# Windowed attention with global tokens and a gated MLP on one core: 512-token chunks, one chunk of all global tokens, clipped band matmuls, denominators from ones columns and exp(-ln), loads in the order of first use

## The chip, the cores and the metric

The kernel runs on one core of one Trainium2 chip. The metric is device time in microseconds (us) of one execution. Each execution has a state (fast or slow); only fast runs are compared. The engines are PE (TensorE: matmuls), PEld (PE's weight loads), DVE (VectorE), ACT (ScalarE), POOL (GpSimd, which also issues the casting loads) and SP (SyncE, which issues plain DMAs).

## The reference, cut to what matters

Eight batches of eight heads. 512 local tokens attend within 32 positions and to 32 global tokens; the global tokens attend to everything. An MLP with the gate h * clip(h + 3, 0, 6) / 6 follows on all 8 x 544 = 4352 tokens.

```python
batch, n_heads, seq_l, seq_g, head_dim = (8, 8, 512, 32, 64)
n_tokens, d_model, d_ff = (4608, 512, 2048)       # w_in 512x2048, w_out 2048x512
k_all = np.concatenate([k_g, k_l], axis=2); v_all = np.concatenate([v_g, v_l], axis=2)
out_g = np.matmul(sm(scale * np.matmul(q_g, k_all.transpose(0, 1, 3, 2))), v_all)
mask = np.abs(pos[:, None] - pos[None, :]) <= 32
s_ll = np.where(mask, scale * np.matmul(q_l, k_l.transpose(0, 1, 3, 2)), -1e9)
s_lg = scale * np.matmul(q_l, k_g.transpose(0, 1, 3, 2))
out_l = np.matmul(sm(np.concatenate([s_lg, s_ll], -1)), np.concatenate([v_g, v_l], axis=2))
x = concat([out_g, out_l], axis=2), tokens in rows # 4352 x 512
h = x @ w_in;  y = (h * np.clip(h + 3.0, 0.0, 6.0) / 6.0) @ w_out
```

## The kernel before

A pair of heads goes through transposes of q and k, QK by key block of 128, exp on ACT, masks on DVE, and the value matmuls ("AV"). The MLP of the batch before is cut into pieces (`fill()`) and put between. Cuts are marked `# ...`.

The value matmuls take all 512 columns of a zero-padded band tile, and two of the seven per head have only 32 rows (the global keys). The kernel splits 544 tokens into a 512-column matmul and a second, 32-column one (`pavB`, here and `psB` below):

```python
def emit_head_av(b, h8, gkE, par):
    # ...
    for kb in range(NKB):
        nc.tensor.matmul(out=pavA[0:MW, 0:SB], lhsT=vn[kb][:, vcol:vcol + MW],
                         rhs=etile[par][kb][:, e * S:e * S + SB], start=(kb == 0), stop=False)
    nc.tensor.matmul(out=pavA[0:MW, 0:SB], lhsT=vg[0:Sg, vcol:vcol + MW],
                     rhs=gkE[0:Sg, 0:SB], start=False, stop=True)
    nc.tensor.matmul(out=pavB[0:MW, 0:SR], lhsT=vn[NKB - 1][:, vcol:vcol + MW],
                     rhs=etile[par][NKB - 1][:, e * S + SB:e * S + S], start=True, stop=False)
    nc.tensor.matmul(out=pavB[0:MW, 0:SR], lhsT=vg[0:Sg, vcol:vcol + MW],
                     rhs=gkE[0:Sg, SB:S], start=False, stop=True)
```

One ones column of `vn` gives the softmax denominator as one row. It is transposed, inverted, transposed back, written to DRAM and read back broadcast over 64 partitions; every second head's result then takes one more DMA to its place:

```python
    nc.vector.transpose(out=dt[D:D + 32, :], in_=xtu[D:D + 32, :])
    nc.vector.reciprocal(out=dt16[...][:, :, 0:1], in_=dt[...][:, :, 0:1])
    nc.vector.transpose(out=rec[D:D + 32, :], in_=dt16[D:D + 32, :])
    nc.sync.dma_start(out=rscr[gi:gi + 1, :], in_=rec[D:D + 1, 0:S])
    # ... later:
    nc.sync.dma_start(out=rbc, in_=rscr[gi:gi + 1, :].to_broadcast([D, S]))
    nc.vector.tensor_tensor(out=xth[:, 0:S], in0=rbc, in1=xtu[0:D, 0:S], op=mult)
    nc.sync.dma_start(out=st["xt"][hp][D:2 * D, 0:S], in_=xth[:, 0:S])
```

The MLP runs per batch over 544 tokens. The second layer has five token tiles, the last of 32 tokens:

```python
for m_ in range(NP):                                    # first layer, 16 column blocks c
    nc.tensor.matmul(out=psA[:, 0:SB], lhsT=lhs, rhs=st["xt"][m_][:, 0:SB], ...)
    nc.tensor.matmul(out=psB[:, 0:SR], lhsT=lhs, rhs=st["xt"][m_][:, SB:S], ...)
# ... relu and gate, once for psA and once for psB
for c in range(NDFF):                                   # second layer, NTS = 5 token tiles
    nc.tensor.matmul(out=po[0:ntok, 0:dm], lhsT=gts[c][:, t0:t0 + ntok], rhs=w_out_t[c], ...)
```

All weights are loaded ahead of batch 0's q, k and v, on one queue (POOL's).

The softmax here doesn't subtract the row's maximum and nothing guards it: scores larger than these inputs give would overflow.

## Time and profile before

| | before |
|---|---|
| median of 4 executions | 566.08 us (564.65 to 577.32; the highest counts as slow, 2.2% above the fastest; the mean of the other three is 565.6) |
| profiled execution: span, mean granted PE clock | 567.9 us, 0.930 |
| first PE matmul | 38.5 us |
| PE idle after that | 57.5 us |

The page gives each engine's busy time and share; its clock row is PE's granted clock in tenths of full speed, in 40 slices.

```profile
span 567.9 us, 9070 instructions
...
PE 471.9 (83%) x3072; PEld 222.2 (39%) x3072; DVE 345.3 (61%) x913; ACT 274.8 (48%) x705; POOL 168.8 (30%) x408
...
PEclk9999969999797997989699997979979998999799
```

PE is the busiest engine by far. The waits view (engine, waiting instruction, what it waited for: us in total, times, longest) says where PE stood still, with the long first wait on top:

```profile
PE psq L173 <- DMA qgb<-in_q_g_dram: 38.5, 1, 38.5
PE psA L304 <- DMA xt_5522<-xth: 5.8, 1, 5.8
PE psA L304 <- DMA xt_2954<-xth: 2.6, 1, 2.6
```

The `xt` waits come at the end of the reciprocal's trip through DRAM: the first MLP matmuls of a batch need the last pair's result. There is one such wait in nearly every batch.

PE's timeline (start us, duration us, engine, line, output<-inputs, weight rows*columns, moving shape) during one head's value matmuls. Going from a matmul with 128 weight rows to one with 32, or back, is called a tiling change below. Durations overlap, so read the distance from one start to the next:

```profile
248.52 0.38 PE L249 MATMUL pavA<-E_0_107,vn_2059 128*96 128x512 f16 x1
...
249.16 0.38 PE L249 MATMUL pavA<-E_3_113,vn_2083 128*96 128x512 f16 x1
249.47 0.41 PE L252 MATMUL pavA<-gkE,vg 32*96 32x512 f16 x1
249.82 0.22 PE L254 MATMUL pavB<-E_3_113,vn_2083 128*96 128x32 f16 x1
249.96 0.21 PE L257 MATMUL pavB<-gkE,vg 32*96 32x32 f16 x1
250.11 0.39 PE L326 MATMUL po<-wout_153,gt_2634 128*128 128x512 f16 x1
250.33 0.38 PE L326 MATMUL po<-wout_155,gt_2650 128*128 128x512 f16 x1
```

512-wide matmuls follow each other at 0.215 us. Around the 32-row ones it is different: 249.16 to 249.47 is 0.31, 249.47 to 249.82 is 0.35, and the two 32-wide ones take 0.14 and 0.15 us.

Last, the windows view (stretch, length, busy us and count of PE, PEld, DVE, ACT, POOL, then PE's clock, DMA share, GB/s). PE falls to half clock after a thin stretch (attention with no MLP work between; even so, no gap between PE's matmuls from 60 us to there is longer than 0.8 us) and stays there for some 9 us although it is 100% busy:

```profile
76.00:78.00 2.00, 2.00 (x6) 0.69 (x5) 1.17 (x3) 1.97 (x7) 1.32 (x9) 0.50 1.90 136
...
80.00:82.00 2.00, 2.00 (x9) 0.94 (x9) 1.97 (x7) 0.67 (x2) 0.00 (x0) 0.50 0.23 60
```

I summed this over the whole trace in windows of 2 us. "Clock loss" is PE's busy time times (1 - clock), and "full-clock busy" is what is left. PE's idle time is the span less the time to the first PE work and less PE's busy time.

| kernel | span | first PE work | PE idle after it | clock loss | full-clock busy |
|---|---|---|---|---|---|
| before | 567.9 | 38.5 | 57.5 | 34.7 | 437.2 |

### The profile page before, as it was taken

The page shows a single profiled execution, that of the slowest core. Times are in us where ns is not written, and L with a number is a line of the kernel's source. Part 1 is how long each engine was busy: PE and PEld are TensorE (multiplying, and loading weights), DVE is VectorE, ACT ScalarE, POOL GpSimd, SP SyncE. Part 2 cuts the span into 40 slices and gives each one's busy share as a digit, 9 for nine tenths or more (in the row PEclk, how much of TensorE's full clock was granted, in tenths as well). Part 3 has the DMA queues.
Part 4 walks back from the last instruction along what each step waited for, and adds up shares of the span by engine and source line. Part 5 has one row for each costly group of instructions (what it writes and reads, how often), then busy time and mean ns, then how long its engine had stood idle before and what let it go on. Part 6 is the DMA issues. An engine that isn't in the chain of part 4 may idle for free.

```text
span 567.9 us, 9070 instructions
## 1 busy us (share of the span) xinstructions
PE 471.9 (83%) x3072; PEld 222.2 (39%) x3072; DVE 345.3 (61%) x913; ACT 274.8 (48%) x705; POOL 168.8 (30%) x408
## 2 busy tenths in 40 slices
PE   0028898998798987999988987989979988999597
PEld 0013444444343443444444443434434443444243
DVE  9004787846684476853778466843868546873551
ACT  0016857706583076813577075830758156840350
POOL 8796741605133051511316051330511011010000
PEclk9999969999797997989699997979979998999799
DMA  6999990926139260861609260391600110002001
GB/s 108 198 152 75 89 85 21 95 71 64 25 30 85 76 55 16 62 68 64 51 21 96 70 64 25 37 89 65 56 20 17 57 38 25 16 30 70 17 20 61
DMA packets 122095, 33.83 MB, mean 60 GB/s; under 512 B 108928, under 2 KB 117184, under 8 KB 122048
## 3 DMA queue, kind: packets, MB, share of 16 engines
q0 software_dynamic: 109248, 17.57, 41.3%
q1 hardware_dynamic: 12800, 15.68, 9.1%
q8 instruction: 24, 0.39, 0.3%
q14 instruction: 23, 0.19, 0.1%
HBM read 39.58 MB, written 8.98 MB: 86 GB/s over the span
## 4 chain that ended last, share of the span: by engine, by line
PE 55%; DVE 19%; DMA 12%; ACT 7%; POOL 4%; issue 2%; SPq 0%; POOLq 0%; ACTq 0%; DVEq 0%
PE po L326 25%; PE pavA L249 10%; PE psA L304 10%; DMA rbc<-rscr 7%; DVE rec L273 4%; PE pavA L252 3%; DVE dTh_140 L267 2%; DMA rscr<-rec 2%; DVE xth L289 2%; DMA win_151<-in_moe_w_in_dram 2%; ACT etmp L212 1%; ACT kT L189 1%; ACT qT L180 1%; PE psGA L226 1%; PE pavB L254 1%
## 5 line engine op out<-in xcount | busy, mean ns | idle before, releaser
L180 ACT COPY qT<-psq 128x544 f16<-128x544 f16 x32 | 19.6, 612 | 136.5 <-PE psq L176 136.5
L219 POOL COPY E_0_107<-etmp 128x32 f16<-128x32 f16 x32 | 9.1, 283 | 234.3 <-ACT etmp L212 234.0
L329 DVE COPY ot<-po 128x512 f32<-128x512 f32 (+1 forms) x40 | 27.6, 689 | 83.6 <-PE po L326 83.6
L173 PE MATMUL psq<-ident,qgb 32*128 32x32 f16 x32 | 5.9, 183 | 38.5 <-DMA qgb<-in_q_g_dram 38.5
L233 ACT ACTIVATE gkE<-psGA 32x512 f16<-32x512 f32 x64 | 36.2, 576 | 0.0
L216 DVE TENSOR_TENSOR E_0_107<-etmp,mask_95 128x192 f16<-128x192 f16 x32 | 8.1, 254 | 39.9 <-issue 27.2
L252 PE MATMUL pavA<-gkE,vg 32*96 32x512 f16 x64 | 28.6, 446 | 0.0
L304 PEld LDWEIGHTS <-win_151 128*128 128x128 f16 x128 | 13.2, 103 | 38.0 <-DMA xt_5522<-xth 6.1
L273 DVE STREAM_TRANSPOSE rec<-dTh_1_143 32x544 f16<-32x544 f16 x32 | 23.2, 726 | 0.8
L273 DVE STREAM_TRANSPOSE rec<-dTh_0_141 32x544 f16<-32x544 f16 x32 | 23.1, 723 | 0.6
L204 PEld LDWEIGHTS <-kT 64*128 64x128 f16 x256 | 11.2, 95 | 25.6 <-ACT kT L189 18.1
L173 PEld LDWEIGHTS <-qgb 32*128 32x128 f16 x32 | 3.4, 105 | 45.0 <-DMA qgb<-in_q_g_dram 38.5
L304 PEld LDWEIGHTS <-win_147 128*128 128x128 f16 x128 | 13.4, 105 | 18.1 <-issue 5.2
L304 PEld LDWEIGHTS <-win_149 128*128 128x128 f16 x128 | 13.2, 103 | 18.2 <-issue 5.2
L189 ACT COPY kT<-psk 128x544 f16<-128x544 f16 x32 | 19.9, 620 | 0.2
L263 ACT COPY xtu_133<-pavA 65x512 f32<-65x512 f32 x8 | 4.7, 582 | 31.6 <-PE pavA L252 31.6
L154 POOL DMA_DIRECT2D qgb<-in_q_g_dram x8 | 4.8, 598 | 47.2 <-PE psq L176 47.2
L252 PEld LDWEIGHTS <-vg 32*96 32x96 f16 x64 | 7.6, 119 | 28.2 <-issue 28.2
L208 PEld LDWEIGHTS <-kT 64*128 64x128 f16 x256 | 14.4, 103 | 9.1 <-issue 8.9
L219 POOL COPY E_0_115<-etmp 128x32 f16<-128x32 f16 x32 | 8.7, 273 | 30.8 <-ACT etmp L212 30.7
L304 PEld LDWEIGHTS <-win_145 128*128 128x128 f16 x128 | 12.7, 99 | 11.6 <-issue 2.5
L226 PE MATMUL psGA<-qT,kT 64*32 64x512 f16 x64 | 14.1, 436 | 0.0
(1772 smaller groups left out, 1777.0 us busy)
## 6 DMA issues: line engine op xcount, KB each, us to landing
out_dram<-ot SPq DMA_DIRECT2D x32, 256.0 KB
rbc<-rscr SPq DMA_DIRECT2D x64, 68.0 KB
rscr<-rec SPq DMA_DIRECT2D x64, 1.1 KB
win_145<-in_moe_w_in_dram POOLq DMA_DIRECT2D x1, 512.0 KB, 5.8
win_147<-in_moe_w_in_dram POOLq DMA_DIRECT2D x1, 512.0 KB, 5.3
win_149<-in_moe_w_in_dram POOLq DMA_DIRECT2D x1, 512.0 KB, 6.6
win_151<-in_moe_w_in_dram POOLq DMA_DIRECT2D x1, 512.0 KB, 8.5
out_dram<-ot SPq DMA_DIRECT2D x8, 64.0 KB
```

The source lines that it names most:

```text
L180: nc.scalar.copy(out=qT, in_=psq[:, 0:S])
L189: nc.scalar.copy(out=kT, in_=psk[:, 0:S])
L208: nc.tensor.matmul(out=psS[e][:, c0 + Sg:c0 + BW], lhsT=lhs, rhs=qT[e * D:(e + 1) * D, Sg + F[kb]:Sg + F[kb] + FR])
L219: nc.gpsimd.tensor_copy(out=etile[par][kb][:, e * S:e * S + Sg], in_=etmp[:, c0:c0 + Sg])
L226: nc.tensor.matmul(out=psGA[e][0:Sg, 0:SB], lhsT=kT[e * D:(e + 1) * D, 0:Sg], rhs=qT[e * D:(e + 1) * D, 0:SB])
L233: nc.scalar.activation(out=gkE[0:Sg, 0:SB], in_=psGA[e][0:Sg, 0:SB], func=EXP, scale=qk_scale)
L249: nc.tensor.matmul(out=pavA[0:MW, 0:SB], lhsT=vn[kb][:, vcol:vcol + MW], rhs=etile[par][kb][:, e * S:e * S + SB], start=(kb == 0), stop=False)
L252: nc.tensor.matmul(out=pavA[0:MW, 0:SB], lhsT=vg[0:Sg, vcol:vcol + MW], rhs=gkE[0:Sg, 0:SB], start=False, stop=True)
L273: nc.vector.transpose(out=rec[D:D + 32, :], in_=dt16[D:D + 32, :])
L304: nc.tensor.matmul(out=psA[:, 0:SB], lhsT=lhs, rhs=st["xt"][m_][:, 0:SB], start=(m_ == 0), stop=(m_ == NP - 1))
L326: nc.tensor.matmul(out=po[0:ntok, 0:dm], lhsT=gts[c][:, t0:t0 + ntok], rhs=w_out_t[c], start=(c == 0), stop=(c == NDFF - 1))
L329: nc.vector.tensor_copy(out=ot[0:ntok, :], in_=po[0:ntok, 0:dm])
```

## The change

The intent: take columns and instructions off PE, take the DRAM trip out of the chain, and start earlier. The diff replaces nearly the whole body; this is its core (cuts marked).

```diff
-        for kb in range(NKB):
-            nc.tensor.matmul(out=pavA[0:MW, 0:SB], ..., rhs=etile[par][kb][:, e * S:e * S + SB], ...)
-        nc.tensor.matmul(out=pavA[0:MW, 0:SB], lhsT=vg[0:Sg, ...], rhs=gkE[0:Sg, 0:SB], ...)
+            # vgz: all 128 rows, zero outside the head's 32; columns 64..127 are ones
+            nc.tensor.matmul(out=pav[:, 0:Sl], lhsT=vgz[:, b, h], rhs=EG[:, 0:Sl], start=True, ...)
+            nc.tensor.matmul(out=pg[:, m, e], lhsT=vgz[:, b, h], rhs=EG[:, Sl:S], start=True, ...)
+            for kb in range(NT):
+                lo, w = WIN[kb]                         # w is 160 or 192
+                nc.tensor.matmul(out=pav[:, lo:lo + w], lhsT=vn[b % NV][:, kb, h],
+                                 rhs=E[:, e, half, COL[kb]:COL[kb] + w], ...)
+                nc.tensor.matmul(out=pg[:, m, e], lhsT=vn[b % NV][:, kb, h],
+                                 rhs=E[:, e, half, g0:g0 + Sg], ...)
-        nc.vector.transpose(...); nc.vector.reciprocal(...); nc.vector.transpose(...)
-        nc.sync.dma_start(out=rscr[gi:gi + 1, :], in_=rec[D:D + 1, 0:S])    # and back, broadcast
+            nc.scalar.activation(out=Ln[e * D:(e + 1) * D], in_=pav[D:P, 0:Sl], func=LN)
+        nc.scalar.activation(out=Rc, in_=Ln, func=EXP, scale=-1.0)
+            nc.vector.tensor_tensor(out=xts[b][m][r], in0=Rc[r], in1=pavs[e][0:D, 0:Sl], op=mult)
# ...
+    emit_globals(0)                                   # globals: loaded once, transposed once
+    for p in range(NPAIR):
+        # T(p + 2), QK(p + 1), AV(p), with 8 MLP units between them
+        if m == NM - 1:
+            units += moe_units(lambda mm, b=b: xts[b][mm], Sl, ...)           # 512 tokens
+    units += moe_units(lambda mm: xg[mm].rearrange("p b s -> p (b s)"), B * Sg, ...)  # 256 globals
# ... loads: k, q of heads 0 to 3, globals, v, the other heads, batch 1, w_in, w_out;
# ... DVE fills vn (ones), kgz and vgz (zeros) before it casts the globals
```

64 ones columns in the value weights give each denominator on 64 PSUM partitions, so no broadcast is needed.

## The prediction

> **What bounds it now.** TensorE. The page's busy table gives PE 83%, DVE 61%, ACT 48%. The waits view: PE's first matmul waits 38.5 us for the q_g load, which is issued after all the weights; later PE waits are short (2 to 6 us per batch for xt after the reciprocal's round trip through DRAM; all PE idle after the start is about 57 us). The windows view shows clock 0.50 in stretches (75 to 85, 175 to 180 us) that follow thin attention phases or waits; the mean is 0.93, so about 30 us are lost to it.
>
> Start-to-start distances in PE's timeline at full clock: 512-wide matmuls 0.216 us; the 32-wide psB one only 0.03; 0.14 to 0.34 where the row tiling changes (a 32-row gkE matmul followed by a 128-row one: 0.34 instead of 0.22). The Trainium skill, TensorEngine Tiling, Key Properties, says that changing the mode drains the engine; the trace agrees with about 0.1 us. Sum: po 640 x 0.216 = 138; psA/psB 126; AV 64 x 1.6 = 102; transposes, QK, G 32 x 1.8 = 58. Together 424 us, + 38 start + clock 30 + gaps = 568.
>
> **What changes on PE (estimates from those distances).**
> - MoE: 8 chunks x 27.7 + one 256-token global chunk 14 = 235 us, instead of 264.
> - AV: one 512-wide, four 160/192-wide, five 32-wide matmuls per head, all 128 rows: about 0.7 us, 45 us in all (was 102).
> - Transposes 0.5, QK 0.65 with its mode changes, G 0.28 per pair: 46 us (was 58).
> Sum about 326: 98 us fewer, all on the limiting engine.
>
> **Other engines.** The DRAM round trip, vector transposes, reciprocals and POOL copies go. Added per pair: two Ln and one Exp (about 0.5 us each by the spacing of 512-wide ACT work), masks 352 wide. With 8 first-layer units, a pair costs about 8.6 us on ACT, 7.8 on DVE, 9.8 on PE: still PE-bound, but ACT is near. Stalls: 10 us.
>
> **Start.** DVE zeroes and fills vn, kgz, vgz before the global casts that PE's first instruction needs. The Trainium skill, VectorE: DVE Perf Modes, Zero memsets, says one cycle per element; the trace of before has no large memset to test it. That is about 19 us of memsets and 5 of ones (estimate from that page), after masks at about 10 us: PE starts at about 30 us. The v_g loads wait for the vgz memsets, and batch 1's loads and w_in queue behind them on POOL (0.9 us each 1024-row load). Batch 0 has no MoE to fill with: ACT-bound, 4 x 4.5 us plus prologue. First MoE matmul at about 58 us.
>
> **Sum.** 58 + 7 batches x 39.5 + tail (last batch 27.7, globals 14, ends 4) + stalls 10 = about 390 us, 0.69 of before. Range 368 to 424. Faster by over 2%: 0.98; within 2%: 0.01; slower: 0.01.
>
> **Right or wrong would show as:** PE busy share over 85% from 60 us to the end, clock near 1.0 there; pair period about 9.8 us in the timeline; AV distances 0.03 for the 32-wide matmuls and 0.07 to 0.08 for the band ones (if weight loads limit them, nearer 0.06 and 0.10: +10 us); PE's first wait released by DVE's casts or memsets at about 30 us; no PE waits on xt from DMA.
>
> **What could be wrong:** memsets two or four times faster than one element per cycle (−8 to −12 us); PSUM's seven shared buffers or the in-order Ln/Exp/multiply chain stalling PE in first-layer stretches (+20 to +30 us); the clock falling to 0.5 there; the dependency tracking making the first transposes wait for all heads' loads (+5 us); late weights (+5 to +15 us).

## The result, and the profile after

| | before | after |
|---|---|---|
| median of 4 executions | 566.08 us | 375.88 us (375.38 to 376.71) |
| profiled span, clock | 567.9 us, 0.930 | 375.0 us, 0.986 |

The ratio is 0.6645, 95% interval 0.6628 to 0.6662. A ratio here is the mean time of one kernel's fast runs over that of the other's in the same rounds, so it is not quite the ratio of the medians. The prediction of 390 us, range 368 to 424, holds.

The page after, the same lines:

```profile
span 375.0 us, 6707 instructions
...
PE 332.3 (89%) x2608; PEld 178.9 (48%) x2608; DVE 235.6 (63%) x489; ACT 239.5 (64%) x473; POOL 102.6 (27%) x132
...
PEclk9998969999999999999999999999999999999999
```

PE's clock row now shows dips only in its first six slices. PE's waits after:

```profile
PE psGT L190 <- DVE kgn_192 L183: 20.1, 1, 20.1
PE pg L286 <- DVE xg_199 L314: 4.7, 6, 0.8
PE psH L324 <- DMA win_86<-in_moe_w_in_dram: 2.1, 1, 2.1
```

No wait on `xt` from DMA is left. The first wait is released by DVE, at 20.1 us. One head's value matmuls in PE's timeline after:

```profile
107.82 0.38 PE L284 MATMUL pav<-EG,vgz 128*128 128x512 f16 x1
108.03 0.18 PE L286 MATMUL pg<-EG,vgz 128*128 128x32 f16 x1
108.06 0.23 PE L292 MATMUL pav<-E,vn_83 128*128 128x160 f16 x1
108.13 0.18 PE L295 MATMUL pg<-E,vn_83 128*128 128x32 f16 x1
108.16 0.24 PE L292 MATMUL pav<-E,vn_83 128*128 128x192 f16 x1
...
108.44 0.18 PE L295 MATMUL pg<-E,vn_83 128*128 128x32 f16 x1
108.47 0.38 PE L324 MATMUL psH<-xt_732,win_84 128*128 128x512 f16 x1
```

From 107.82 to 108.47 a head takes 0.65 us, where it took about 1.6 before (248.52 to 250.11 for the head shown). Band matmuls are 0.07 to 0.08 apart, and the 32-wide ones, with a full weight load each, only 0.03. Two windows, batch 0's attention and one steady batch:

```profile
23.00:45.00 22.00, 16.56 (x221) 11.59 (x217) 13.06 (x34) 21.19 (x55) 18.05 (x26) 0.92 1.58 143
...
85.00:125.00 40.00, 38.49 (x312) 20.46 (x311) 25.92 (x57) 28.47 (x55) 10.51 (x12) 1.00 0.69 67
```

Batch 0, with no MLP to fill with, is bound by ACT (21.19 of 22 us). In the steady batch PE is busy for 38.49 of 40 us at full clock. The second layers of successive batches start 40.2 us apart (70.4, 110.6, 150.8 us).

| kernel | span | first PE work | PE idle after it | clock loss | full-clock busy |
|---|---|---|---|---|---|
| before | 567.9 | 38.5 | 57.5 | 34.7 | 437.2 |
| after | 375.0 | 20.1 | 22.6 | 4.7 | 327.6 |
| difference | 192.9 | 18.4 | 34.9 | 30.0 | 109.6 |

The four differences add up to the gain: 57% of it is full-clock busy time of PE, the rest is waiting, half clock and the start. Full-clock busy is not work alone. The experiment a7 below runs the same 2608 matmuls as the kernel after, and its full-clock busy is 11.5 us higher, in batches that have more waits. So up to some 10 us of the 109.6 may be of that kind and not work taken away.

### The profile page after: what moved, and what is told of

It is laid out like the page before. It is cut to its first block, busy times and chain, and to the rows that moved or that the text cites. A ratio compares the mean times of both kernels' runs of the same rounds, so it can differ in the third digit from the quotient of the medians.

```text
span 375.0 us, 6707 instructions
## 1 busy us (share of the span) xinstructions
PE 332.3 (89%) x2608; PEld 178.9 (48%) x2608; DVE 235.6 (63%) x489; ACT 239.5 (64%) x473; POOL 102.6 (27%) x132
## 4 chain that ended last, share of the span: by engine, by line
PE 62%; DVE 12%; POOL 9%; ACT 9%; issue 3%; DMA 3%; POOLq 0%
PE po L338 27%; PE psH L324 23%; PE pav L292 4%; ACT Rc L301 3%; DMA win_86<-in_moe_w_in_dram 3%; ACT Ln L298 3%; PE pav L284 2%; POOL kn L103 2%; POOL qn L103 2%; PE psGA L256 2%; POOL vn_81 L107 1%; POOL vgz L161 1%; PE pg L295 1%; POOL kn L96 1%; POOL qn L96 1%
## 5 line engine op out<-in xcount | busy, mean ns | idle before, releaser
L298 ACT ACTIVATE Ln<-pav 64x512 f32<-64x512 f32 x64 | 37.9, 593 | 45.4 <-PE pav L292 38.1
L342 DVE COPY ot<-po 128x512 f32<-128x512 f32 x34 | 23.5, 692 | 25.6 <-PE po L338 25.2
L96 POOL DMA_DIRECT2D kn<-in_k_l_dram x28 | 24.7, 898 | 44.3 <-PE psT L213 36.5
L219 ACT COPY qT<-psT 128x512 f16<-128x512 f16 x32 | 18.8, 586 | 22.9 <-DVE kT L218 22.7
L96 POOL DMA_DIRECT2D qn<-in_q_l_dram x28 | 24.8, 926 | 6.7 <-PE psH L324 1.9
L284 PE MATMUL pav<-EG,vgz 128*128 128x512 f16 x64 | 24.7, 386 | 1.4 <-ACT qT L219 1.1
L244 DVE TENSOR_TENSOR E<-E,mask_79 128x352 f16<-128x352 f16 x64 | 19.8, 337 | 8.4 <-ACT E L242 8.2
L244 DVE TENSOR_TENSOR E<-E,mask_80 128x352 f16<-128x352 f16 x64 | 20.9, 340 | 5.4 <-ACT E L242 3.4
L324 PEld LDWEIGHTS <-win_86 128*128 128x128 f16 x144 | 14.2, 98 | 18.4 <-DMA win_86<-in_moe_w_in_dram 2.4
L301 ACT ACTIVATE Rc<-Ln 128x512 f32<-128x512 f32 x32 | 20.0, 626 | 0.7
L112 POOL DMA_DIRECT2D vn_82<-in_v_l_dram x12 | 10.6, 918 | 31.4 <-PE pg L295 31.4
L190 PE MATMUL psGT<-ident,kgn_192 128*128 128x128 f16 x8 | 1.2, 304 | 20.1 <-DVE kgn_192 L183 20.1
L218 DVE COPY kT<-psT 128x512 f16<-128x512 f16 x32 | 13.4, 418 | 2.9 <-PE psT L213 2.9
L112 POOL DMA_DIRECT2D vn_81<-in_v_l_dram x8 | 7.1, 909 | 21.1 <-PE pg L295 20.6
```

Source lines behind the costliest of these rows:

```text
L96: nc.gpsimd.dma_start(out=t[:, kb], in_=src[b, :, kb * P:(kb + 1) * P, :].rearrange("h s d -> s h d"))
L112: nc.gpsimd.dma_start(out=vn[b % NV][:, kb, :, 0:D], in_=v_l[b, :, kb * P:(kb + 1) * P, :].rearrange("h s d -> s h d"))
L219: nc.scalar.copy(out=qT, in_=psT[:, Sl:2 * Sl])
L244: nc.vector.tensor_tensor(out=E[:, e, half, 0:HALF], in0=E[:, e, half, 0:HALF], in1=mask[half], op=mult)
L284: nc.tensor.matmul(out=pav[:, 0:Sl], lhsT=vgz[:, b, h], rhs=EG[:, 0:Sl], start=True, stop=False, skip_group_check=True)
L298: nc.scalar.activation(out=Ln[e * D:(e + 1) * D], in_=pav[D:P, 0:Sl], func=LN)
```

## The experiments

My theory was: PE is the limit, so columns, tiling changes and waits removed from PE count one to one; load order and the DRAM trip matter where PE waits. The rivals were that PE's savings are given back (to waits, to the clock, to ACT and DVE), and that the small parts cost nothing. Names with b edit the kernel before, names with a undo or alter one part of the kernel after. All runs were correct. They ran on three chips, four kernels on each. The kernel before was slower there in its fast runs than in the first measurement (mean 570.6 us on the first of these chips, 571.4 on the second) and on the third only 2 of its 7 runs were fast; so I read the b runs from their ratio to it (the ratios of b2 to b4 imply a mean of about 573.9 us for it; against the 570.6 us, b1 to b4 gain 1.4, 7.0, 3.0 and 6.2%), and for the a runs I compare the times with the 375.88 us of the kernel after, which was measured in an earlier job whose chip is not recorded, so a difference of 1% between an a kernel and it means nothing. Each a kernel's four runs agree within 1%.

| kernel | median us | ratio to before [95%] | first PE | PE idle after | clock loss | full-clock busy |
|---|---|---|---|---|---|---|
| b1_loads_first | 564.34 | 0.9834 [0.9751, 0.9917] | 22.2 | 69.3 | 28.7 | 437.8 |
| b2_clipped | 530.88 | 0.9245 [0.9204, 0.9286] | 38.8 | 46.0 | 29.5 | 415.4 |
| b3_rows128 | 553.08 | 0.9642 [0.9599, 0.9686] | 45.9 | 69.1 | 27.6 | 410.8 |
| b4_all_three | 535.40 | 0.9329 [0.9283, 0.9375] | 29.8 | 82.5 | 29.2 | 394.0 |
| a1_chunks544 | 409.10 | 0.7161 [0.7117, 0.7205] | 20.1 | 20.6 | 4.3 | 362.1 |
| a2_fullwidth | 412.82 | 0.7227 [0.7185, 0.7269] | 20.1 | 21.8 | 2.3 | 366.8 |
| a4_rows32 | 384.70 | 0.6736 [0.6695, 0.6777] | 20.1 | 15.5 | 8.4 | 339.0 |
| a7_dram_trip | 410.01 | 0.7171 [0.7119, 0.7223] | 20.1 | 40.4 | 9.5 | 339.1 |
| a3_weights_first | 390.78 | 0.6815 [0.6762, 0.6868] | 20.6 | 33.2 | 4.3 | 330.8 |
| a5_reciprocal | 495.89 | 0.8637 [0.8550, 0.8725] | 20.1 | 83.8 | 46.6 | 344.6 |
| a6_opening | 374.71 | 0.6536 [0.6476, 0.6595] | 12.7 | 27.3 | 5.3 | 329.5 |
| a8_opening_win | 378.92 | 0.6609 [0.6556, 0.6662] | 12.7 | 32.0 | 4.2 | 329.0 |

### a1_chunks544: the 544-token chunks back

```diff
+                nc.tensor.matmul(out=ps2[:, 0:Sg], lhsT=w_in_t[m][:, c * P:(c + 1) * P], rhs=rhsg(m), ...)
+            # relu and gate of the 32 columns; a fifth output tile of 32 tokens
-    units += moe_units(... all globals ...)
```

> Kernel after, with MoE chunks of 544 tokens again (each batch's 32 global tokens as a second PSUM tile and a fifth, 32-token output tile; no chunk of all globals). Theory (PE-bound): 8 x (64 x 0.03 + 16 x 0.216) - 14 = +29 us, about 405 us. Rival (the doubled small ACT and DVE instructions make ACT the limit in first-layer stretches): +45 us or more, with PE waiting on DVE's gt there.

It measured 409.1 us, 33 more than the kernel after (29 expected). Full-clock busy rose by 34.5 and PE's idle time did not (20.6 against 22.6). This is the theory's outcome: the doubled small ACT and DVE instructions cost PE only a few us of waits, while the fifth output tile and the 32-column matmuls are paid in full.

### a2_fullwidth: the band's columns back, on PE alone

```diff
+                for z0, z1 in ((0, lo), (lo + w, Sl)):
+                    if z1 > z0:
+                        nc.tensor.matmul(out=pav[:, z0:z1], lhsT=vn[b % NV][:, kb, h],
+                                         rhs=zt[:, 0:z1 - z0], start=False, stop=False, ...)
```

> Kernel after, with each band value matmul followed by matmuls of zeros over the rest of the 512 columns: same result, PE columns as without clipping, no work added on another engine. Theory (PE-bound): 64 heads x 1344 columns x 0.417 ns = +36 us, about 412 us. Rival (PE's idle time absorbs part): under +20 us.

It measured 412.8 us, 37 more (+36.0 in the spans, against 36 expected). Full-clock busy rose by 39.2. In the kernel after, a column on PE costs what a column takes. That the total met the estimate so closely is partly luck: clock loss fell by 2.4, and a wait of 3.6 us for the new tile of zeros (`pav<-zt` on POOL), a side effect of the edit, stood against smaller waits elsewhere.

### b2_clipped: the same part, alone, in the kernel before

```diff
+        nc.tensor.matmul(out=pavA[0:MW, 0:SB], lhsT=vg[0:Sg, ...], rhs=gkE[0:Sg, 0:SB], start=True, ...)
         for kb in range(NKB):
-            nc.tensor.matmul(out=pavA[0:MW, 0:SB], ...)
+            c0, c1 = Sg + F[kb], min(Sg + F[kb] + FR, SB)
+            nc.tensor.matmul(out=pavA[0:MW, c0:c1], ..., rhs=etile[par][kb][:, e * S + c0:e * S + c1], ...)
+            nc.tensor.matmul(out=pavA[0:MW, 0:Sg], ..., rhs=etile[par][kb][:, e * S:e * S + Sg], ...)
```

> Kernel before, with the value matmuls clipped to the band (192 or 160 columns plus 32 global ones, instead of 512) and nothing else changed. Theory (PE-bound, matmul columns count one to one): 64 heads x 4 x (0.216 - 0.08 - 0.03) us = -27 us, about 539 us. Rival (the thinner attention phases leave PE waiting on ACT, DVE and the DRAM trip, or at half clock): -13 us or less, with PE idle or clock-loss grown by the rest.

It came out 7.5% faster (spans: -38.2 us), more than the expected 27 us. Full-clock busy fell by 21.8, a little less than estimated, but idle time fell by 11.5 and clock loss by 5.2 as well. The rival, that thinner attention would wait more, is refuted. PE's waits:

```profile
PE psA L308 <- DMA xt<-xth: 11.1, 7, 6.3
```

Its waits on `xt` are 11.1 us in all; in the kernel before they are about 19. What made the waits shorter here is not settled: the edit also changes the order of the value matmuls.

### b3_rows128: no 32-row matmuls, in the kernel before

```diff
-            gkE = wrk.tile([Sg, S], FP16, tag="gkE", name="gkE", bufs=6)
+            gkE = gkz[(2 * pidx + e) % 6]              # [P, S], zeroed once; vg likewise
-                         lhsT=vg[0:Sg, vcol:vcol + MW], rhs=gkE[0:Sg, 0:SB], ...
+                         lhsT=vg[:, vcol:vcol + MW], rhs=gkE[:, 0:SB], ...
```

> Kernel before, with the 32-row matmuls of the global keys (gkE, vg) padded with zero rows to 128 rows: same columns, four tiling changes per head fewer. Theory (each change of row tiling drains PE for 0.1 us): 64 heads x 0.44 us = -28 us, about 538 us; the timeline's distances around these matmuls fall from 0.31/0.34/0.15/0.14 to 0.22/0.22/0.03/0.03. Rival (no cost of its own, the distances are weight loads): distances and time unchanged.

PE's timeline shows the cost of the tiling changes gone (349.99 to 350.20 is 0.21, then 0.03; the kernel before had 0.35, then 0.14):

```profile
349.99 0.38 PE L262 MATMUL pavA<-gkz,vgp 128*96 128x512 f16 x1
350.20 0.18 PE L264 MATMUL pavB<-E,vn 128*96 128x32 f16 x1
350.23 0.20 PE L267 MATMUL pavB<-gkz,vgp 128*96 128x32 f16 x1
```

Full-clock busy fell by 26.4 us, as the theory had it. The time fell by only 3.6% (spans: -14.5 us). Two things took the rest: zeroing the tiles on POOL delayed the first loads (first PE work at 45.9 us instead of 38.5; a side effect of my edit), and the waits on `xt` grew:

```profile
PE psA L314 <- DMA xt<-xth: 30.6, 9, 6.5
```

### b1_loads_first: load order alone, in the kernel before

```diff
-    # w_in, w_out loads                                 (before any of batch 0's)
+    emit_loads(0)
+    # w_in, w_out loads
```

> Kernel before, with batch 0's q, k, v loads issued ahead of the weights and nothing else changed. Theory (load order is worth what it takes off PE's first wait): first PE matmul at about 21 us instead of 38.5, time about 549 us (-17). Rival (the start is absorbed by later waits for weights or by batch 0's thin phase): within 4 us of before.

It was 1.7% faster, the interval reaching from 0.8 to 2.5%; one of its four runs was slow, and by the 2% that the record asks for the verdict is unclear. The spans differ by 9.9 us, of which 6.0 is less clock loss. PE did start at 22.2 us, 16.3 earlier; but a new wait of 10.7 us took most of it back:

```profile
PE pavA L250 <- POOL E L220: 10.7, 1, 10.7
```

POOL's timeline around it (the bracket says what ended the idle time before an instruction):

```profile
20.20 2.18 POOL L162 DMA_DIRECT2D win<-in_moe_w_in_dram  x4
...
27.73 0.53 POOL L167 DMA_DIRECT2D wout<-in_moe_w_out_dram  x1 [3.24 <-DMA win<-in_moe_w_in_dram]
...
40.85 2.06 POOL L220 COPY E<-etmp 128x32 f16<-128x32 f16 x12
```

POOL copies the global columns of the exponentials and also issues the loads, in order. Its copies for the first pairs stood behind the weight loads, which themselves waited for earlier ones to land. So the rival was half right: the start was worth 16 us, and a wait on the engine that issues the loads absorbed 11 of them. The kernel after has no such copies on POOL.

### b4_all_three: the three together

> Kernel before with the three edits of the sibling runs together (load order, clipped band, 128-row globals). Theory (PE-bound, savings add): -72 us, about 494 us. Rival (waits for the reciprocal's DRAM trip, and the clock, take part of it back): 510 us or more, with PE's waits on xt from DMA grown.

The three parts together (535.4 us) are not faster than clipping alone (530.9). Full-clock busy fell by 43 us and PE started 8.7 earlier, yet idle time grew by 25. PE's waits and one of them in the timeline:

```profile
PE psA L319 <- DMA xt<-xth: 35.1, 9, 6.6
```

```profile
265.78 0.18 PE L321 MATMUL psB<-xt,win 128*128 128x32 f16 x1
270.87 0.61 PE L319 MATMUL psA<-xt,win 128*128 128x512 f16 x1 [4.92 <-DMA xt<-xth]
...
271.34 0.59 PE L319 MATMUL psA<-xt,win 128*128 128x512 f16 x1
```

The wait for `xt` is 4.9 us in this batch and 35.1 us in all, 24 more than with clipping alone. Two other waits are new: 7.2 us for batch 1's `q_g` load, and 4.9 for the copies on POOL, as in b1; and the zeroing on POOL, from b3, puts the start 7.6 us later than in b1. After the wait shown, a pair of 512 and 32 columns takes 0.46 us, at half clock. The clock loss as a whole did not grow, though (29.2 us; 34.7 in the kernel before, 29.5 with clipping alone): what took the savings back is idle time. This is the rival's outcome as to the waits, not as to the clock: work taken off PE turned into waits, most of them for the DRAM trip. That the trip sets the boundary here is read from the waits; no run took the trip out of the kernel before.

### a7_dram_trip: the DRAM trip back, in the kernel after

```diff
-        Rc = wrk.tile([P, Sl], FP32, tag="Rc", name="Rc", bufs=2)
+        Rc = wrk.tile([P, Sl], FP16, tag="Rc", name="Rc", bufs=2)
+            nc.sync.dma_start(out=rscr[gi:gi + 1, :], in_=Rc[e * D:e * D + 1, :])
+            nc.sync.dma_start(out=rbc[r], in_=rscr[gi:gi + 1, :].to_broadcast([D, Sl]))
+        # multiply by rbc instead of Rc
```

> Kernel after, with the reciprocals written to DRAM and read back broadcast, as the kernel before did, 5 to 6 us more before each multiply. Theory (once per batch the next batch's MoE waits for the last pair's xt): 8 x about 3.5 us = +28 us, about 404 us, PE waits on xt or on DVE at each batch's start. Rival 1 (other work hides it): under +8 us. Rival 2 (value tiles held in PSUM longer stall every pair): +60 us or more.

It measured 410.0 us, 34 more; "hidden" and "stalls every pair by 60 us" are both refuted. The size was near (28 expected), the place only partly. The first second-layer matmul comes 13.7 us later (84.1 instead of 70.4 us), because each of batch 0's pairs waits for a trip; seven batches then take 20.5 us more (292.5 instead of 272.0), about 3 each. PE's waits show the expected one on `xt`, and others as large further on:

```profile
PE psH L332 <- DVE xt L312: 7.9, 9, 1.6
PE pav L287 <- DVE xt L312: 7.1, 6, 3.3
```

In idle time, clock loss and full-clock busy the 34.1 us are 17.8, 4.8 and 11.5. So the trip is paid in the kernel after too.

### a4_rows32: a 32-row matmul back, in the kernel after

```diff
+            g = slice(pos(h) * Sg, (pos(h) + 1) * Sg)
-            nc.tensor.matmul(out=pav[:, 0:Sl], lhsT=vgz[:, b, h], rhs=EG[:, 0:Sl], ...)
+            nc.tensor.matmul(out=pav[:, 0:Sl], lhsT=vgz[g, b, h], rhs=EG[g, 0:Sl], ...)
```

> Kernel after, with the 512-wide global value matmul on 32 rows (row tiling) instead of 128 zero-padded ones: two tiling changes more per head. Theory (0.1 us per change): 64 x 0.2 = +13 us, about 389 us. Rival (no cost): within 3 us of after.

It measured 384.7 us, 9 more (13 expected). PE's timeline (x3 is three matmuls in a row, 0.216 us apart, so the last starts at 106.01):

```profile
105.58 0.81 PE L325 MATMUL psH<-xt,win 128*128 128x512 f16 x3
106.32 0.38 PE L285 MATMUL pav<-EG,vgz 32*128 32x512 f16 x1
106.64 0.24 PE L293 MATMUL pav<-E,vn 128*128 128x160 f16 x1
```

From the 32-row matmul to the next is 0.32 us, 0.10 more than the 0.22 without it. Entering costs as much: from the last MLP matmul to the 32-row one is 0.31 us (0.310 to 0.312 before all 56 heads that an MLP matmul precedes), where it is 0.216 in the kernel after. So both changes cost what was expected. Full-clock busy rose by 11.4 us and clock loss by 3.7; idle time fell by 7.1 (the wait for w_in by 2.3, a steady batch's idle time by 0.3). A steady batch takes 1.38 us longer, PE being busy 1.67 us longer in it. Of this cost, then, a part went into waits that were there before.

### a3_weights_first: weights first again, in the kernel after

```diff
     make_identity(nc, ident)
+    # w_in, w_out loads
     load_qk(0, True)
```

> Kernel after, with the weight loads issued first, as the kernel before did. Theory (first loads are on the path): k and q land at about 28 us instead of 10, batch 0 ends about 12 us later, the 3 us wait for w_in goes: +8 to +12 us, about 386 us. Rival (the start is bound by DVE's memsets at 20 us, not by loads): within 3 us of after.

It measured 390.8 us, 15 more, somewhat over the expected 8 to 12. PE's waits name the cause:

```profile
PE psT L213 <- DMA kn<-in_k_l_dram: 13.7, 6, 10.2
```

The load order is worth its time even though DVE holds the very first matmul.

### a5_reciprocal: DVE's reciprocal instead of Ln and Exp on ACT

```diff
-            nc.scalar.activation(out=Ln[e * D:(e + 1) * D], in_=pav[D:P, 0:Sl], func=LN)
+            nc.vector.reciprocal(out=Rc[e * D:(e + 1) * D], in_=pav[D:P, 0:Sl])
-        nc.scalar.activation(out=Rc, in_=Ln, func=EXP, scale=-1.0)
```

> Kernel after, with DVE's reciprocal of the 64x512 denominators in PSUM instead of ACT's Ln and Exp. Theory ([...]17 elements took 240 ns in the kernel before): 4.3 us each, 64 of them, DVE 235 + 275 = 510 us busy, time 520 us or more, DVE-bound. Rival (one cycle an element): 0.65 us each, time within 5 us of after.

It measured 495.9 us, 120 more. The costliest group of DVE's instructions (busy us, mean ns of one):

```profile
L297 DVE RECIPROCAL Rc<-pav 64x512 f32<-64x512 f32 x64 | 215.1, 3360 | 3.0 <-PE pav L291 1.0
```

One takes 3.36 us, about 6.3 cycles per element at the 0.96 GHz that the Trainium skill gives for this engine ("VectorE: DVE Perf Modes", "Specifications"); I had said 4.3 us, which is 8 cycles per element at that clock. The same page, section "First, the fixed hardware budget", says that a reciprocal repeats a divide step 8 times; it does not say what an element costs. The trace shows that one cycle an element is refuted, and that 8 is too many. DVE is busy for 444 of 495 us. Ln and Exp cost ACT 0.59 us per head and 0.63 per pair, and ACT has room.

### a6_opening and a8_opening_win: an earlier start

```diff
-    for i in range(NV):
-        nc.vector.memset(vn[i][:, :, :, D:P], 1.0)     # now on ACT
# globals cast before vgz is zeroed; their copies on DVE, their loads on two queues
     load_qk(1, False)
+    # w_in                                             (a8: ahead of load_qk(1))
     load_v(1)
```

> Kernel after, opening mended: vn's ones written by ACT, which is idle then, the globals loaded from two queues, their copies moved from ACT to DVE, w_in ahead of batch 1's v. Theory (start bound by DVE's 12.8 us of memsets and 4.5 of ones; batch 0 bound by ACT): PE starts at about 14 us instead of 20, first MoE matmul at about 39 instead of 45.7, time about 368 us. Rival (w_in's landing binds): within 2 us of after, with the wait for w_in grown.

> As a6_opening, but w_in also ahead of batch 1's q and k. If w_in's landing bound a6_opening: 2 to 5 us faster than it. If batch 1's k and q bind instead: the same or slower, PE waiting on the transposes of batch 1.

a6 started PE at 12.7 us, 7.4 earlier, and was not measurably faster: 374.7 against 375.9 us, from different jobs, with spans of 374.9 and 375.0. Its first MLP matmul came at 45.25 us, against 44.68. a8, from the same job as a6, was 4.2 us slower than a6 (378.34 to 379.70 against 373.09 to 376.60). Waits of a6:

```profile
PE psGT L192 <- DVE kgn L143: 12.7, 1, 12.7
...
PE psT L215 <- DMA qn<-in_q_l_dram: 4.9, 6, 2.0
```

The transposes of batch 1 now wait for its k and q. The page's DMA row of the kernel after shows the DMA engines at 90% or more of their time for the first 10 of 40 slices (94 us):

```profile
DMA  9999999999390469119961949100001000100202
```

My theory of the opening (bound by DVE, then ACT) falls, and so does its rival (bound by w_in alone). DVE does hold the first matmul; but the end of the opening is held by the loads, whichever goes first. In a6, k and q of batch 1 come late; in a8 w_in goes first and they come later still, with a 9.3 us wait on k (the outcome that a8's expectation gave for this case). How much ACT alone would have allowed in a6 stays open. No version that clearly beats the kernel after was found.

## Why the prediction was right or wrong, point by point

- **PE bounds both kernels: right for the kernel after,** where columns put back cost their time in full (a2: +36.0 us against 36). In the kernel before it held only in part: b3 took 26.4 us off PE's full-clock busy time and b4 43, and their spans fell by 14.5 and 32.4.
- **PE work, 424 to 326 us: the second is right, the first too small.** Full-clock busy is 327.6 after and 437.2 before. The gain from this term was 109.6 us, not 98, with the reserve made above; the 424 does not enter the predicted 390 us.
- **The value matmuls at about 0.7 us per head; the 32-wide ones 0.03, the band ones 0.07 to 0.08 apart: right** (0.65 us; 0.03; 0.07 to 0.08). Weight loads do not limit them.
- **Tiling changes cost about 0.1 us each: right,** for leaving a 32-row matmul (0.10 in a4, 0.13 in the kernel before) and for entering one (0.09 to 0.10 in both).
- **The start: this step failed.** "PE starts at about 30 us"; it started at 20.1. What was wrong is the time that DVE needs before PE's first instruction. DVE's timeline (a bracket gives idle time before):

```profile
1.51 1.76 DVE L149 MEMSET vn_81<- 128x2048 f16 x1 [0.38 <-issue]
3.65 1.76 DVE L149 MEMSET vn_82<- 128x2048 f16 x1 [0.38 <-issue]
...
7.94 1.76 DVE L150 MEMSET kgz<- 128x2048 uint32 x1 [0.38 <-issue]
10.50 3.47 DVE L151 MEMSET vgz<- 128x4096 uint32 x1 [0.80 <-issue]
...
19.23 0.79 DVE L183 CAST kgn_192<-kgn 128x1024 f16<-128x1024 f32 x1
```

  The ones of `vn` run at one element per cycle: 2048 elements, 2.14 us from start to start. But the zero fills of `kgz` and `vgz` were carried out as 32-bit writes of half as many elements (128x2048 uint32 for 4096 two-byte ones). The section of the Trainium skill's "VectorE: DVE Perf Modes" that I cited, "Zero memsets can be issued as uint32 (trn2)", says that this can be done, and I had not applied it: the fills of `vn`, `kgz` and `vgz` together took 12.5 us (1.51 to 13.97), not 19. The prediction had named faster memsets as a risk of 8 to 12 us. And the masks, put at 10 us in front of them, did not come first: the instructions were put on DVE in another order than the source has them, with the mask copies at 13.89 us.
- **Batch 0 bound by ACT: right** (21.19 of 22 us), 24.6 us from PE's start to the first MLP matmul, against the 28 implied. That matmul came at 44.7 us instead of 58; nearly all of the 14 us that the whole prediction was too high lie here. It then waited about 3 us for w_in.
- **39.5 us per batch plus stalls: right** (40.2). ACT was near enough to show, and DVE too, only in waits of 0.3 us.
- **The tail of about 46 us: right.** 49 us remain after seven batches from 44.7 us (44.7 + 7 x 40.2 = 326.1 us).
- **The clock: right.** About 30 us lost before, 4.7 after.
- **What the prediction did not see** is how the parts depend on each other. In the kernel before, clipping, tiling and loads together gave no more than clipping alone (b4 and b2); the waits, most of them for the DRAM trip, took the rest. The change gained from all its parts; that this is because it also took out the trip fits the waits and the 34 us of a7, but no run shows it: none took the trip out of the kernel before.

What stays open: the parts put back one at a time (a1, a2, a3, a4, a7) cost 128 us together, of a gain of 190, and the rest was not taken apart; why clipping alone shortened the waits in the kernel before, and why that kernel's fast runs scatter (559.7 to 576.0 us over the kernel before and b1) where the kernel after repeats within 0.4%.

## What to carry to other kernels

Where one engine is the limit, add up its work as distances between starts at full clock, and keep waits and clock loss apart: the sum predicts the time only once both are small. Test each part of a large change in the kernel that you have and in the one that you get: a part can give back its gain in the first (a wait that was hidden becomes the limit) and be worth all of it in the second. Before tuning the first microseconds, see whether the loads would allow an earlier end of the opening at all.

## What the Trainium skill lacked or had wrong

- "TensorE: Matmul & The Clock Gate", section "Back-to-back issue gap": it gives about 131 ns per matmul for a sustained stream of weight loads and 512-wide matmuls. Here such a stream runs at 215 to 216 ns (250.11 to 250.33 us in the kernel before), which is the figure that the page gives for an isolated gap; at 32 columns with full weight loads it is 25 to 30 ns.
- The same page, "What's actually happening": it says that the clock comes back after about 3.4 us of sustained work. In the kernel before PE was 100% busy at clock 0.50 from 76 to 84 us, 8 us long. In the kernel after it was so from 50 to 54 us, which the page still allows, as it says that the window runs free of the kernel. The two levels, half and full, agree.
- "TensorEngine Tiling (Array Packing)", "Key Properties": it says that a change of mode drains the engine, without a size. Leaving a 32-row matmul cost 0.10 us (a4) to 0.13 us (before), entering one 0.09 us (before) to 0.10 us (a4).
- "VectorE: DVE Perf Modes": no rate is given for the reciprocal. 512 elements per partition from PSUM took 3.36 us. The memset rates of "Zero memsets can be issued as uint32 (trn2)" agree with the trace (2048 elements in 2.14 us).
- No page that I read warns that an engine which issues loads and also computes holds up its compute behind load issues that wait for earlier loads: 10.7 us in b1.
